# A Mamba-2 scan followed by top-1 routed experts: six routing groups, late scatters spread over two jobs, the first job begun ahead of the last rows

## The chip, the core and the metric

The kernel runs on one core of a Trainium2 chip. The metric is the device time of one execution in microseconds (us); lower is better. PE is the matrix engine (TensorE; its weight loads are listed apart as PEld), DVE the vector engine, ACT the scalar engine, POOL the general-purpose engine (GpSimd), SP the engine that here only issues DMAs. PE's results go to PSUM; SBUF is the on-chip working memory and HBM the large one.

## What is computed

```
# Mamba-2 scan, batch 4, 8 heads, sequence 768, head 32, state 16, in chunks:
y[i] = sum_{j<=i in chunk} (C_i . B_j) * decay(i,j) * x_j  +  (C_i . state) * decay(i)
state = decay_chunk * state + sum_j B_j x_j * decay(j..end)

x = y as (3072 tokens, 256)
logits = x @ w_gate                       # 8 experts
e = argmax(logits); gate = softmax(logits)[e]
out = gate * ( relu(x @ w1[e]) @ w2[e] )  # 256 -> 1024 -> 256
```

## The kernel before

The program has two parts. The first, the scan, works on 24 units of 128 tokens, two to a step, in a loop over twelve steps `d`. The second, the experts, works on jobs: eight jobs of 256 tokens, one to each expert, and then four pairs of smaller jobs for the tokens that did not fit. Between them stands the routing: each token's row (its 256 values, logits by parts, token number) is scattered into the HBM tensor `x_hbm`, at a place in its expert's region, and every job loads its rows from there.

The order on every engine is the order in which the code is written; no scheduler changes it. Each engine runs its own list in order and waits by semaphores for the others.

One step `d` of the scan does this on PE: the state's part of the output (`y_old`), the chunk's part (`y_own`, one matmul for each head, its right side the masked scores `M` that DVE makes in `weigh`, its left side `xp` that POOL makes in `scaled_x`), and the scores of the next step (`scores`). ACT copies the output from PSUM (`turned`, tile `yT`). One step later `rows` turns it back to rows of tokens on PE and `rows_out` and `logits_of` (DVE) write rows and logits. For the last two steps, 10 and 11, `rows` stands behind the loop, before the first job.

A routing group is a number of units that are ranked together. `RGS` gives the sizes, `CUT` the number of groups that the first scatters belong to; the last group is scattered late. When a group's logits are known, `choose` and `count` mark the experts (DVE and POOL), `rank` counts places on PE in the next step, and `ranked` (DVE) writes the places `pos`. `place(k)` scatters unit `k`: an indirect DMA that POOL issues (line 414), with a one-element memset of the tile `spare` (line 413) ahead of it where `apart` is set. The list `todo` holds the units that wait for it; the loop takes units from it at fixed points of a step.

`m_load(i)` loads a job's rows: five DMAs that SP issues, into `xb` (four) and `lt`. They read `x_hbm`, so they wait for every scatter ahead of them to land. `m_xT(i)` transposes `xb` on DVE into `xT`. `m_h(i)` makes the 1024 hidden values in eight blocks `f`, two matmuls each on PE into one of four PSUM buffers, and a relu on ACT from there into `hT`; after each block it calls `between(f)`, which holds the other work of that time. `m_y(i)` makes the two 128-token halves of the output on PE; ACT scales each by its gate (`put`, tile `yo`) and POOL scatters it to the output (line 553). `load_w(e, u, q)` loads a quarter of an expert's weights through SP. `over` (in job 1) counts all groups, and `empty_rest` scatters empty rows behind the last ones.

Of the kernel before, what the change touches and what calls it, by code (L numbers as in the profile page):

```python
# [23 lines left out]
ND = NP * NC  # L24
NU = 2 * ND
AMIN = 0.75
RGS = [4, 4, 4, 4, 8]
CUT = 4
LAST = len(RGS) - 1
R0 = [sum(RGS[:i]) for i in range(len(RGS))]  # L30
# [17 lines left out]
def ssd_then_moe(ctx, tc, xs_in, ae_in, wgx, w_gate, w1, w2, gx, gb, gc, ga, out):  # L48
    nc = tc.nc
# [152 lines left out]
    def load_w(e, u, q):  # L202
        n = KT * F // 4
        nc.sync.dma_start(out=w_sb[e][u][:, q * n:q * n + n], in_=(w1, w2)[u][e, :, q * n:q * n + n])
# [213 lines left out]

    def place(k, apart=True):
        to_places(rt[grp[k]][:, k - R0[grp[k]], :], pos[:, k:k + 1], apart)  # L420
# [136 lines left out]
    def put(p, mid, gt, dve):  # L557
        yo = mo.tile([128, DM], FP32, name="yo", bufs=3)
        if dve:
            nc.vector.tensor_scalar(out=yo, in0=p, scalar1=gt, scalar2=None, op0=ALU.mult)  # L560
        else:
            nc.scalar.mul(yo, p, gt)  # L562
        put_out(yo, mid)
# [6 lines left out]
    def m_y(i, pp):  # L570
        e = jobs[i][1]
        for t in range(2 - jobs[i][0]):
            p = y_next()
            for f in range(FT):
                nc.tensor.matmul(p, lhsT=ex[i]["hT"][:, f, 128 * t:128 * t + 128],  # L575
                                 rhs=w_sb[e][1][:, f * DM:f * DM + DM], start=(f == 0), stop=(f == FT - 1))
            put(p, ex[i]["lt"][:, t], ex[i]["g"][:, t:t + 1], i >= E - 1)

# [122 lines left out]
    with tc.manual_schedule():  # L701
# [36 lines left out]
        wq = [0, 0, 0, 0, 1, 2, 3, 4, 5, 6, 7, 8]  # L738
        for d in range(ND):
# [7 lines left out]
            per = 3 if d == 8 else 2  # L747
            while todo and d == 10:
                place(todo.pop(0))
# [4 lines left out]
            if todo and d < 10:  # L754
                place(todo.pop(0), False)
                if d == 8:
                    place(todo.pop(0))
            if d + 1 < ND:
                for s in range(2):
                    masked_C(2 * d + 2 + s)  # L760
                    scaled_x(2 * d + 2 + s, nc.gpsimd)
            faded(d)
            if k >= 0:
                if d < ND - 1:
                    rows(k)
# [35 lines left out]
            if k >= 0 and d < ND - 1:  # L801
                rows_out(k)
                if d == 4:
                    take_totals(1)
            if d == 0:
                route_consts()
            if k >= 0 and d < ND - 1:
                logits_of(k)
# [12 lines left out]
            if d == 9:  # L821
                for _ in range(2):
                    place(todo.pop(0))
            if d == 10:
                m_load(0)
                m_load(1)
            if d == 9:
                weakest()
        rows(ND - 2)
# [6 lines left out]
        for e, u in ((1, 1), (2, 0), (2, 1)):  # L836
            for k in range(4):
                load_w(e, u, k)
        rows(ND - 1, Y)
        rows_out(ND - 2)  # L840
        logits_of(ND - 2)
        m_xT(0)
        rows_out(ND - 1, Y)
        logits_of(ND - 1)
        choose(LAST)
        count(LAST)
        for i in range(E):
            def between(f):
                if f == 1:
                    ex[i]["g"] = gates(ex[i]["lt"], 2)  # L850
                if i == 0:
                    if f == FT // 2:
                        rank(LAST)
                        ranked(LAST)
                        for k in range(R0[LAST], NU):
                            place(k)
                        m_load(2)
                        m_load(3)
                    return
                if f != FT // 2:  # L860
                    return
# [20 lines left out]
            if i < E - 1:  # L882
                m_y(i, pp)
# [79 lines left out]
```

## Time and profile before

| | us |
|---|---|
| median of 3 runs | 260.78 (260.47 to 261.06) |
| the profiled execution, its own time | 259.0 |
| its span, first to last instruction | 257.3 |
| PE busy within the span | 240.2 (93%) |
| DVE, ACT, POOL busy | 88.0, 87.7, 84.1 (33 to 34%) |

The page of a profile has each engine's busy time and the span in 40 slices. The timeline lists an engine's instructions in order of time, runs of like ones merged: start, length, engine, line, operation, what is written and read, how many, and in brackets the idle time of the engine ahead of it with what ended it. A matmul of 32-bit values stands as two records. The view by stretches gives for each stretch the busy time of every engine and the clock that PE was granted (1.00 is 2.4 GHz, 0.50 is 1.2 GHz).

### The profile page before, as it was taken

What the parts mean: (1) busy time and instruction counts of PE and PEld (TensorE: products, weight loads), DVE (VectorE), ACT (ScalarE), POOL (GpSimd) and SP (SyncE); (2) the same over time, 40 slices, a digit from 0 to 9 for tenths busy, and PEclk for the clock granted to TensorE, in tenths of its full rate; (3) what the DMA queues carried; (4) which work ended last, traced back from release to release, by engine and by line L of the source; (5) the groups of instructions that cost most, each with busy time, mean ns of one, the idle gap of its engine ahead of it and who ended that gap; (6) DMA issues with size and microseconds to landing.
All of it is one profiled execution on the core that took longest, in us unless ns stands there. A gap on an engine that the chain in (4) does not pass through costs nothing. (4 is left out here: it accounts for less than half of the span.)

```text
span 257.3 us, 5473 instructions
## 1 busy us (share of the span) xinstructions
PE 240.2 (93%) x2013; PEld 202.3 (79%) x2013; DVE 88.0 (34%) x274; ACT 87.7 (34%) x288; POOL 84.1 (33%) x147
## 2 busy tenths in 40 slices
PE   7899899876899879999999999999999999999992
PEld 5677667653688668888888888888998968989781
DVE  5899786845660050202020200106204204222000
ACT  4566647540032041414132322223060431523300
POOL 3745868872018704241413203030201301313031
PEclk9999999996899999999999999999999999999999
DMA  6999968524793389696958597413221200101001
GB/s 172 322 378 323 339 216 247 202 84 103 206 319 122 125 176 327 151 298 146 299 165 265 170 288 176 73 32 73 55 60 29 68 4 16 46 8 38 3 15 43
DMA packets 36407, 39.75 MB, mean 154 GB/s; under 512 B 21947, under 2 KB 23806, under 8 KB 36352
## 3 DMA queue, kind: packets, MB, share of 16 engines
q1 hardware_dynamic: 33360, 30.37, 41.5%
q0 software_dynamic: 2880, 8.66, 8.9%
q8 instruction: 27, 0.44, 0.7%
q14 instruction: 28, 0.23, 0.3%
q10 hardware_dynamic: 112, 0.05, 0.1%
HBM read 29.72 MB, written 9.86 MB: 154 GB/s over the span
## 5 line engine op out<-in xcount | busy, mean ns | idle before, releaser
L540 PE MATMUL h_ps<-xT,w 128*128 128x256 f32 (+3 forms) x512 | 90.1, 335 | 3.3 <-ACT hT L549 2.5
L540 PEld LDWEIGHTS h_ps<-xT,w 128*128 128x128 f32 x512 | 80.6, 190 | 10.9 <-ACT hT L549 2.9
L575 PE MATMUL y_ps<-w,hT 128*128 128x256 f32 x384 | 85.0, 380 | 0.0
L575 PEld LDWEIGHTS y_ps<-w,hT 128*128 128x128 f32 x384 | 72.6, 190 | 10.5 <-issue 0.8
L553 POOL DMA_INDIRECT out_dram<-yo,lt x24 | 23.8, 991 | 76.7 <-ACT yo L562 41.5
L498 DVE TENSOR_REDUCE t_se<-t_sub 128x1 f32<-128x8 f32 (+1 forms) x20 | 3.3, 165 | 115.6 <-ACT t_sub L496 115.6
L549 ACT ACTIVATE hT<-h_ps 128x256 f32<-128x256 f32 x64 | 24.1, 384 | 32.9 <-PE h_ps L540 27.3
L278 DVE TENSOR_TENSOR M<-g,mask 128x1024 f32<-128x1024 f32 x24 | 28.3, 1219 | 12.0 <-PE g L273 7.9
L414 POOL DMA_INDIRECT x_hbm<-rows,pos x24 | 23.8, 992 | 9.6 <-issue 3.6
L615 ACT ACTIVATE hT<-h_ps 128x128 f32<-128x128 f32 (+2 forms) x64 | 18.0, 292 | 23.8 <-PE h_ps L540 23.0
L562 ACT ACTIVATE yo<-y_ps,t_gt 128x256 f32<-128x256 f32 x14 | 6.6, 474 | 43.9 <-PE y_ps L575 36.6
L331 PE MATMUL y<-M,xp 128*32 128x128 f32 x384 | 16.6, 292 | 4.7 <-DVE M L278 3.9
L331 PEld LDWEIGHTS y<-M,xp 128*32 128x32 f32 x384 | 11.4, 115 | 8.5 <-POOL xp L266 3.4
L336 ACT COPY yT<-y 128x512 f32<-128x512 f32 x12 | 7.0, 586 | 29.5 <-PE y L331 27.9
L343 PEld LDWEIGHTS r<-turn,yT 128*128 128x128 f32 x88 | 12.2, 189 | 5.5 <-ACT yT L336 3.9
L343 PE MATMUL r<-turn,yT 128*128 128x160 f32 x88 | 14.9, 312 | 1.7 <-ACT yT L336 1.1
L261 ACT ACTIVATE cm<-xs_n,par 128x128 f32<-128x128 f32 x46 | 15.1, 419 | 1.4 <-DMA xs_n<-in_xs_dram 1.4
L266 POOL TENSOR_TENSOR xp<-xs_n,Ei 128x256 f32<-128x256 f32 x23 | 13.7, 618 | 5.1 <-DVE xp L266 3.5
L273 PE MATMUL g<-cm,xs_n 32*128 32x256 f32 x192 | 15.1, 429 | 0.0
L414 POOL DMA_INDIRECT x_hbm<-zrows,rest x8 | 7.7, 964 | 22.2 <-DMA lt<-x_hbm 14.2
L553 POOL DMA_INDIRECT out_dram<-yh,lh x4 | 3.9, 984 | 32.8 <-ACT yh L589 20.9
L560 DVE TENSOR_SCALAR yo<-y_ps,t_gt 128x256 f32<-128x256 f32 x10 | 4.7, 484 | 23.9 <-PE y_ps L575 23.9
(120 smaller groups left out, 148.6 us busy)
## 6 DMA issues: line engine op xcount, KB each, us to landing
w<-in_w_dram SPq DMA_DIRECT2D x64, 256.0 KB
xs_n<-in_xs_dram SPq DMA_DIRECT2D x20, 320.0 KB
xb<-x_hbm SPq DMA_DIRECT2D x32, 64.0 KB
xb<-x_hbm SPq DMA_DIRECT2D x32, 48.0 KB
xs_n<-in_xs_dram SPq DMA_DIRECT2D x4, 192.0 KB
x_hbm<-zrows SPq DMA_DIRECT2D x1, 672.0 KB
lt<-x_hbm SPq DMA_DIRECT2D x8, 80.0 KB
xs_n<-in_xs_dram SPq DMA_DIRECT2D x4, 128.0 KB
```

The lines of the kernel that those rows point to most:

```text
L261: nc.scalar.mul(t[:, u], st[n]["CT"], par[:, u:u + 1])
L266: eng.tensor_tensor(out=t, in0=st[n]["x"].rearrange("p (h d) -> p h d", d=D), in1=bc(Ei[:, n, :, None], [128, NH, D]), op=ALU.mult)
L273: nc.tensor.matmul(g_ps[:, q, n % 2], lhsT=st[n]["BT"][r], rhs=st[n]["cm"][r].rearrange("p u i -> p (u i)"), start=True, stop=True)
L278: nc.vector.tensor_tensor(out=t, in0=g_ps[:, :, n % 2].rearrange("p q (u i) -> p q u i", u=2), in1=bc(mask[:, None, None, :], [128, 4, 2, ...
L331: nc.tensor.matmul(y_ps[o:o + D, h // 4, CH * s:CH * s + CH], lhsT=st[n]["xp"][:, D * h:D * h + D], rhs=st[n]["M"][:, h], start=first, sto ...
L343: nc.tensor.matmul((to[s] if to else r_ps[:, s])[:, 256 * t:256 * t + 160], lhsT=sd[d]["yT"][:, t, CH * s:CH * s + CH], rhs=turn[:, t].rea ...
L414: s_ = nc.gpsimd.indirect_dma_start(out=x_hbm[:, :], out_offset=bass.IndirectOffsetOnAxis(ap=at, axis=0), in_=row, in_offset=None)
L540: nc.tensor.matmul(p[:, 0:n], lhsT=w[:, c:c + 128], rhs=xT[:, t, 0:n], start=(t == 0), stop=(t == KT - 1))
L549: nc.scalar.activation(ex[i]["hT"][:, f, 0:n], q, func=ACT.Relu)
L553: return nc.gpsimd.indirect_dma_start(out=out[:, :], out_offset=bass.IndirectOffsetOnAxis(ap=tok, axis=0), in_=yo[:, :], in_offset=None, b ...
L575: nc.tensor.matmul(p, lhsT=ex[i]["hT"][:, f, 128 * t:128 * t + 128], rhs=w_sb[e][1][:, f * DM:f * DM + DM], start=(f == 0), stop=(f == FT ...
L615: nc.scalar.activation(ex[i + u]["hT"][:, f, 0:n], q, func=ACT.Relu)
```

## The change

`RGS` is cut into six groups in place of five: the fourth group of four units becomes two groups of two, so that one more `rank` runs, in step 8. Units are taken from `todo` up to three times a step from step 8 on; all 16 units of the first groups are then scattered by the end of step 9. The loads for jobs 0 and 1, and those of the weights of expert 2, are issued behind them at the end of step 9; the second weights of expert 1 are loaded ahead of them. `rows` for step 10 moves into step 11, and the transposition for job 0 too. `rows` for step 11 moves behind the first block of job 0. The eight scatters of the last group, which stood together in job 0, are now in pairs: two behind block 5 of job 0, two behind each of its output halves, and two in job 1, behind a small copy on POOL (`behind`) that reads the third block of its `hT`. The loads for jobs 2 and 3 follow the last pair.

```
-RGS = [4, 4, 4, 4, 8]
-CUT = 4
+RGS = [4, 4, 4, 2, 2, 8]
+CUT = 5
...
+    def behind(ap):
+
+        nc.gpsimd.tensor_copy(spare, ap)
...
-    def m_y(i, pp):
+    def m_y(i, pp, then=None):
...
             put(p, ex[i]["lt"][:, t], ex[i]["g"][:, t:t + 1], i >= E - 1)
+            if then:
+                then()
...
-        wq = [0, 0, 0, 0, 1, 2, 3, 4, 5, 6, 7, 8]
+        wq = [0, 0, 0, 0, 1, 2, 3, 4, 5, 6, 7, 8, 9, 9, 9, 9]
...
-            per = 3 if d == 8 else 2
-            while todo and d == 10:
-                place(todo.pop(0))
             if todo:
                 place(todo.pop(0), False)
             if k >= 0:
                 whole(k)
-            if todo and d < 10:
+            if todo:
                 place(todo.pop(0), False)
-                if d == 8:
-                    place(todo.pop(0))
             if d + 1 < ND:
                 for s in range(2):
                     masked_C(2 * d + 2 + s)
                     scaled_x(2 * d + 2 + s, nc.gpsimd)
+            if todo and d > 7:
+                place(todo.pop(0), False)
             faded(d)
             if k >= 0:
-                if d < ND - 1:
-                    rows(k)
+                rows(k)
...
-            if k >= 0 and d < ND - 1:
+            if d == ND - 1:
+                m_xT(0)
+            if k >= 0:
                 rows_out(k)
...
-            if k >= 0 and d < ND - 1:
+            if k >= 0:
                 logits_of(k)
...
             if d == 9:
-                for _ in range(2):
+                while todo:
                     place(todo.pop(0))
-            if d == 10:
                 m_load(0)
                 m_load(1)
-            if d == 9:
+                for k in range(8):
+                    load_w(2, *divmod(k, 4))
+            if d == 10:
                 weakest()
-        rows(ND - 2)
...
-        for e, u in ((1, 1), (2, 0), (2, 1)):
-            for k in range(4):
-                load_w(e, u, k)
-        rows(ND - 1, Y)
-        rows_out(ND - 2)
-        logits_of(ND - 2)
-        m_xT(0)
-        rows_out(ND - 1, Y)
-        logits_of(ND - 1)
-        choose(LAST)
-        count(LAST)
+        left = list(range(R0[LAST], NU))
+
+        def more_places(n):
+            for _ in range(n):
+                place(left.pop(0))
+
...
                 if i == 0:
-                    if f == FT // 2:
+                    if f == 0:
+                        rows(ND - 1, Y)
+                        rows_out(ND - 1, Y)
+                        logits_of(ND - 1)
+                        choose(LAST)
+                        count(LAST)
+                    if f == 5:
                         rank(LAST)
                         ranked(LAST)
-                        for k in range(R0[LAST], NU):
-                            place(k)
-                        m_load(2)
-                        m_load(3)
+                        more_places(2)
                     return
+                if i == 1 and f == 2:
+                    behind(ex[1]["hT"][0:1, 2, 0:1])
+                    more_places(len(left))
+                    m_load(2)
+                    m_load(3)
...
-                m_y(i, pp)
+                m_y(i, pp, (lambda: more_places(2)) if i == 0 else None)
```

On POOL, in steps 9 and 10: `S` is the state of `whole`, `xp` the product of `scaled_x`, the DMAs of line 414 are the scatters, `rows_134` the fourth group's rows. Before, from the first scatter of step 9 on:

```order
L414 DMA x_hbm<-rows_133,pos 28672x336
L314 TENSOR_TENSOR S<-S,fa 128x128
L266 TENSOR_TENSOR xp<-xs_n,Ei 128x256 x2
L413 MEMSET spare 1x1
L414 DMA x_hbm<-rows_134,pos 28672x336
L413 MEMSET spare 1x1
L414 DMA x_hbm<-rows_134,pos 28672x336
L413 MEMSET spare 1x1
L414 DMA x_hbm<-rows_134,pos 28672x336
L413 MEMSET spare 1x1
L414 DMA x_hbm<-rows_134,pos 28672x336
L314 TENSOR_TENSOR S<-S,fa 128x128
```

Four scatters of the fourth group stand in a row here. The same stretch of POOL in the changed kernel, where `rows_134` and `rows_135` are the two groups of two:

```order
L414 DMA x_hbm<-rows_133,pos 28672x336
L314 TENSOR_TENSOR S<-S,fa 128x128
L414 DMA x_hbm<-rows_134,pos 28672x336
L266 TENSOR_TENSOR xp<-xs_n,Ei 128x256 x2
L414 DMA x_hbm<-rows_134,pos 28672x336
L413 MEMSET spare 1x1
L414 DMA x_hbm<-rows_135,pos 28672x336
L413 MEMSET spare 1x1
L414 DMA x_hbm<-rows_135,pos 28672x336
L314 TENSOR_TENSOR S<-S,fa 128x128
```

The scatters that stood four in a row between `xp` and the next `S` are now three, and one has moved ahead of `xp`.

On PE, from the scores of the last step to the first blocks of job 0 (line 273 is `scores`, 323 `y_old`, 331 `y_own`, 343 `rows`, 540 or 544 a block of `m_h`), before:

```order
L273 MATMUL g<-cm,xs_n 128x256 x8
L323 MATMUL y<-xs_n,S 64x128 x8
L331 MATMUL y<-M,xp 32x128 x16
L343 MATMUL r<-turn,yT 128x160 x4
L343 MATMUL y_ps_1202<-turn,yT 128x160
L343 MATMUL y_ps_1203<-turn,yT 128x160
L343 MATMUL y_ps_1202<-turn,yT 128x160
L343 MATMUL y_ps_1203<-turn,yT 128x160
L540 MATMUL h_ps_1199<-xT,w_0_85 128x256 x2
```

Here all `rows` of steps 10 and 11 (into `r` and into `y_ps`) stand between the last `y_own` and the first block. The same stretch of PE in the changed kernel:

```order
L273 MATMUL g<-cm,xs_n 128x256 x8
L343 MATMUL r<-turn,yT 128x160 x4
L323 MATMUL y<-xs_n,S 64x128 x8
L331 MATMUL y<-M,xp 32x128 x16
L544 MATMUL h_ps_1226<-xT,w_0_85 128x256 x2
L343 MATMUL y_ps_1229<-turn,yT 128x160
L343 MATMUL y_ps_1230<-turn,yT 128x160
L343 MATMUL y_ps_1229<-turn,yT 128x160
L343 MATMUL y_ps_1230<-turn,yT 128x160
L544 MATMUL h_ps_1227<-xT,w_0_85 128x256 x2
```

The `rows` of step 10 have moved ahead of the last `y_old`, and those of step 11 behind the first block.

On POOL in jobs 0 and 1 (line 557 is the scatter of an output half, line 421 the copy of `behind`, `rows_136` the last group), the changed kernel has:

```order
L557 DMA out_dram<-yo,lt 3072x256
L413 MEMSET spare 1x1
L414 DMA x_hbm<-rows_136,pos 28672x336
L413 MEMSET spare 1x1
L414 DMA x_hbm<-rows_136,pos 28672x336
L557 DMA out_dram<-yo,lt 3072x256
L413 MEMSET spare 1x1
L414 DMA x_hbm<-rows_136,pos 28672x336
L413 MEMSET spare 1x1
L414 DMA x_hbm<-rows_136,pos 28672x336
L421 COPY spare<-hT_138 1x1
```

Before, all eight scatters of the last group stood ahead of the first output half; now two do, and six follow it.

## Rows read from the trace of the kernel before

**Rows 1.** Page: busy us, share, instructions of each engine; PE's granted clock in 40 slices

```profile
PE 240.2 (93%) x2013; PEld 202.3 (79%) x2013; DVE 88.0 (34%) x274; ACT 87.7 (34%) x288; POOL 84.1 (33%) x147
...
PEclk9999999996899999999999999999999999999999
```

**Rows 2.** Stretches: length; busy us (instructions) PE, PEld, DVE, ACT, POOL; clock; DMA

```profile
60.00:66.50 6.50, 5.84 (x76) 3.89 (x80) 4.26 (x7) 0.59 (x1) 0.00 (x0) 0.50 0.60 109
...
85.40:95.20 9.80, 7.30 (x36) 6.04 (x35) 2.79 (x20) 2.94 (x9) 3.06 (x5) 1.00 0.62 146
95.20:109.00 13.80, 13.80 (x66) 12.15 (x65) 2.48 (x11) 4.13 (x11) 4.07 (x6) 1.00 0.77 234
```

**Rows 3.** Timeline of PE, end of step 9 to the first job

```profile
51.62 0.18 PE L388 MATMUL r<-base_e,ones_bf 1*128 1x32 bf16 x1
...
52.22 1.06 PE L331 MATMUL y<-M,xp 128*32 128x128 f32 x32
53.21 1.15 PE L273 MATMUL g<-cm,xs_n 32*128 32x256 f32 x16
...
55.60 0.67 PE L323 MATMUL y<-xs_n,S 32*64 32x128 f32 x15
57.35 0.26 PE L323 MATMUL y<-xs_n,S 32*64 32x128 f32 x1 [1.08 <-issue]
60.23 2.21 PE L331 MATMUL y<-M,xp 128*32 128x128 f32 x32 [2.62 <-DVE M L278]
62.37 2.09 PE L273 MATMUL g<-cm,xs_n 32*128 32x256 f32 x16
64.39 1.13 PE L323 MATMUL y<-xs_n,S 32*64 32x128 f32 x16
65.90 1.77 PE L331 MATMUL y<-M,xp 128*32 128x128 f32 x32 [0.38 <-DVE M L278]
67.61 1.35 PE L343 MATMUL r<-turn,yT 128*128 128x160 f32 x8
68.80 1.25 PE L343 MATMUL y_ps<-turn,yT 128*128 128x160 f32 x8
70.88 4.58 PE L540 MATMUL h_ps<-xT,w 128*128 128x256 f32 x20 [0.83 <-DVE xT L509]
```

**Rows 4.** Timeline of DVE: the masked scores of step 10

```profile
58.86 2.36 DVE L278 TENSOR_TENSOR M<-g,mask 128x1024 f32<-128x1024 f32 x2 [4.08 <-remote]
```

**Rows 5.** Timeline of POOL: the first and the last of four scatters in a row

```profile
53.06 1.01 POOL L414 DMA_INDIRECT x_hbm<-rows,pos  x1 [0.88 <-DVE less L432]
...
56.91 0.96 POOL L414 DMA_INDIRECT x_hbm<-rows,pos  x1 [0.21 <-issue]
```

**Rows 6.** Timeline of PE: the hidden blocks of job 1

```profile
85.35 3.62 PE L540 MATMUL h_ps<-xT,w 128*128 128x256 f32 x16
91.46 1.13 PE L540 MATMUL h_ps<-xT,w 128*128 128x256 f32 x4 [2.50 <-ACT hT L549]
```

**Rows 7.** Timeline of ACT: second output half of job 0, first blocks of job 1

```profile
86.78 0.47 ACT L562 ACTIVATE yo<-y_ps,t_gt 128x256 f32<-128x256 f32 x1 [4.20 <-PE h_ps L540]
91.03 0.66 ACT L549 ACTIVATE hT<-h_ps 128x256 f32<-128x256 f32 x2 [3.77 <-remote]
```

**Rows 8.** Timeline of POOL: first, last scatter of last group; last output half

```profile
76.73 1.01 POOL L414 DMA_INDIRECT x_hbm<-rows,pos  x1 [3.56 <-DMA w<-in_w_dram]
...
85.66 0.96 POOL L414 DMA_INDIRECT x_hbm<-rows,pos  x1 [0.21 <-issue]
...
88.23 1.00 POOL L553 DMA_INDIRECT out_dram<-yo,lt  x1 [0.30 <-issue]
```

**Rows 9.** Timeline of SP: the first load for job 2

```profile
88.31 1.91 SPq L474 DMA_DIRECT2D xb<-x_hbm  x4
```

**Rows 10.** DMA queues from 88.3 to 92.3: packets, MB, share of 16 engines

```profile
q1 hardware_dynamic: 1343, 0.34, 46.0%
```

**Rows 11.** Timeline of DVE: the transposition for job 2

```profile
94.73 0.71 DVE L509 STREAM_TRANSPOSE xT<-xb 128x512 f32<-128x512 f32 x1
```

## The prediction, made before the changed kernel was run

> **What bounds the kernel now.** I read the page first. PE is busy for 240.2 of 257.3 us and no other engine for more than 88 [rows 1], so what is to be had lies in PE's own idle time and in its slow clock; one slice of PEclk reads 6, the others 8 or 9. Then the stretches [rows 2]: from 95.2 on a job fills PE wholly (13.80 of 13.80), and between 60.0 and 66.5 the granted clock is 0.50, the lower of the two levels (1.2 GHz). Two places are left: the end of the scan, and job 1 (85.4 to 95.2: 7.30 busy of 9.80).
>
> At the end of the scan [rows 3] PE ends the scores of step 9, of which step 10's `M` is made, at 54.36 (53.21 + 1.15), and DVE could then make that `M`. It starts at 58.86, after 4.08 us idle [rows 4]; the bracket says "remote", so no instruction's end explains the release. PE stalls 1.08 us in the middle of `y_old` and then 2.62 for `M`; the clock is low from about 60 to 66.5. Over the same time POOL issues four scatters back to back, from 53.06 to 57.87, 1.28 apart [rows 5]; DVE resumes 0.99 behind the last one's end.
>
> In job 1 PE has filled its four PSUM buffers by 88.97 and waits 2.50 for ACT [rows 6]. ACT was late: its last output half of job 0 starts at 86.78, though PE had it ready at about 85.5, and its first block of job 1, ready by 86.4 (85.35 and four records of 0.22), starts at 91.03, again "remote" [rows 7]. The late blocks lie beside the end of ten scatters in a row on POOL, eight from 76.73 on and two of the output, done at 89.23 [rows 8]. So both holes have one look: PE has finished, the reader learns of it late, and POOL has just issued a run of scatters. That is an inference from coincidence; it is the weakest step.
>
> **The change, part by part.** *One more group.* Step 8 gets one `rank` more. In step 9 the rank and the sixteen `own` matmuls take 0.60 together (51.62 to 52.22) [rows 3], so it costs between 0 and 0.6 of PE; the rank is the larger part of that stretch, and I take +0.35. `choose`, `count` and `ranked` of small tiles go to DVE, which is busy a third of the time; the wait for PE's scores hides them, and without it they would cost their own time, which is under that of the rank's stretch again. `weakest` on DVE moves one step on, in front of a wait for scores as before: nothing.
>
> *The run of scatters in steps 9 and 10.* Before the run POOL sat idle 0.88 for `pos` [rows 5]. The scatter that is moved ahead of `xp` takes 1.0 and some 0.15, so it uses that idle time and sets the rest back by 0.27; three scatters from 53.33 on, 1.28 apart, end at 56.85 in place of 57.87. If DVE is released 0.99 behind that, `M` starts at 57.84: -1.0. Bounds: 0, if it is not the run that holds it; -3.7 (PE's 1.08 and 2.62), if a shorter run holds nothing.
>
> *Clock, `rows` of step 10, start of job 0.* PE's idle time shrinks only to some 2.7 us with one matmul in it, so I take it that the clock falls as before, for 6.5 us. PE starts `y_own` at 59.23. At the low clock it takes 2.14 and the scores 2.02 (steps between starts in [rows 3]), to 63.4. `rows` of step 10, now here, take 1.19 at full clock (67.61 to 68.80); scores slow from 1.1 to 2.02, so I take 2.2, to 65.6. There the clock is full again: `y_old` 0.6 and `y_own` 1.06, to 67.3. DVE's `M` for step 11, started behind the scores, needs 2.36, done by 65.9, and `xT` 0.71 [rows 11], done by 66.6, so neither is waited for. The first block begins at 67.3; `rows` of step 11 (1.25) lie behind it, and ACT's copy for them is hidden by that block's 0.87. Against 70.88 that is 67.3 + 1.25 - 70.88 = -2.4, of which -1.0 is counted above: -1.4. What covers the moved `rows` is the wait for `M` (0.38, and what of it a full clock would add); at the low clock it covers them only in part, and that is in the sum. Behind `xT` on DVE are queued `rows_out` of steps 10 and 11, for which PE waits only at the rank in job 0, six blocks on.
>
> *Loads.* Those for job 0 still follow the last scatter of the run, so they move by the same 1.0, and now lead two megabytes of weights as they led three. The four quarters for expert 1 go to step 9, where SP has nothing else to do. No term.
>
> *Scatters in jobs 0 and 1.* Six of the eight leave the stretch before the first output half. If a run of ten makes PE's news late, and runs that are broken by output scatters don't, the 2.50 of job 1 goes: -2.5; bounds 0 and -2.5. I take all of it, because PE in job 0 stood beside eight scatters without a gap, and only the end of the run was beside a hole.
>
> *What is late next: the rows of job 2.* Count from T1, the start of job 1. A half of `m_y` is 16 records at 0.216, 3.45 [rows 6], and ACT's 0.47 with some 0.3 for hand-over follows, so the first half of job 0 is with POOL about 2.65 before T1. Output scatter 1.3, two scatters 2.55: POOL is free at T1 + 1.2, when the second half waits already; output 1.3, two scatters 2.55, the copy (no row shows it; between 0 and the 0.30 that stands ahead of an output scatter [rows 8], taken 0.15; its block was ready by about T1 + 3.2), two scatters 2.2 to the second one's end: T1 + 7.4. The load waited 1.69 behind the end of the last scatter (86.62 to 88.31) [rows 8, 9], so it is issued at T1 + 9.1. In 4.0 us from there 0.34 MB had moved [rows 10], and one job's `xb` are 0.25, so they land 3.0 to 4.4 behind their issue, and 6.4 at the latest, when DVE transposed them [rows 11]. `xT` is then there at T1 + 12.8 to 14.2; job 1 ends at T1 + 13.9. Before, there were over 6 us to spare; now there is nothing. I take +0.2, between 0 and +2.3 (with 6.4). The copy holds POOL up, and behind it stand two scatters, and through them the loads for jobs 2 and 3 on SP and `empty_rest` on POOL; the last two have a job's time more.
>
> *The sum:* 0.35 - 1.0 - 1.4 - 2.5 + 0.2 = -4.35. The profiled execution would go from 259.0 to 254.65. The median of the timed runs lies 1.8 above it; the same difference gives 256.4.
>
> **The rivals.** *The clock stays up.* The idle time of 2.50 in job 1 left it at 1.00 [rows 2, 6], and the shortened hole is about as long. Against it: before that hole PE had run dense, here it had run in short pieces. At full clock `y_own` waits for its second `M` (to 60.8), scores 1.1, `rows` 1.2, `y_old` 0.6, then `M` again: the first block at 65.2 and not 67.3. That gives 254.3.
>
> *The hole in job 1 stays.* POOL still issues out, two, out, two, two behind each other across T1, with the same 0.3 between them; only the copy has been put in, and it does not wait. Then 2.3 come back (the 0.2 at job 2 is absorbed): 258.7.
>
> *Neither hole has to do with the run.* What speaks for it: from 76.73 to 85.35 PE kept step beside seven scatters. Then only the rank, the moved `rows` and the start of job 0 count, 0.35 - 1.4 = -1.05, and job 1 keeps its hole: 259.7. The Trainium skill ("SBUF — State Buffer", section "SBUF: two separate sides") would have it so: of the engines only DVE and GpSimd share a port, and PE and ACT never wait on anyone. By that rule both hole terms would be 0; the rows neither bear it out nor refute it, since what is late in [rows 4, 7] is the news of PE's work and not a port.
>
> *Slower: job 2 waits.* If `xT` of job 2 comes 2.6 late, PE stands as long as at 57.6 to 60.2, after which the clock fell. Price: 2.6 - 0.2 for the wait and about 3.2 for 6.5 us at half clock: 262.0. It decides from `xb` landing 6.7 behind its issue, or a POOL chain that is longer by as much (ACT's second half of job 0 held up as at 86.78 is 0.7 of that). For it: no slack is left. Against it: 6.4 was the most the landing took before, and the loads of rows then had weights behind them as now.
>
> **How the numbers follow.** Forecast 0.44, clock up 0.15, hole stays 0.17, no link 0.10, slower 0.14. A measurement here tells about 0.2% (0.5 us) from no change. Faster by over that: the first three and half of the fourth, less 0.04 for what I have mispriced, 0.77; within it 0.08; slower 0.15. The likeliest case alone reaches from 254.9 to 258.3. For 8 in 10 the range takes in the clock's case and the hole's and part of the fourth, and ends short of the slower one: 253.5 to 260.4.
>
> **What would show it.** POOL's three scatters ending near 56.9 and `M` starting within 1 us of it; PEclk near 61; the first block of job 0 directly behind the last `y_own`, at about 67, with `rows` behind it; no idle PE in job 1; the start of job 2 on PE, with or without a wait for `xT`. It is wrong if the wait for `M` keeps its place or grows, or if job 2 starts more than 2 us late.

## The result

| | us |
|---|---|
| median after, 6 runs | 252.59 (251.26 to 253.48) |
| median before, 6 runs beside them | 260.68 (259.51 to 261.49) |
| ratio | 0.9689, 95% interval 0.9653 to 0.9726 |
| the profiled execution of after, its own time; its span | 252.05; 250.3 |

The change makes the kernel 3.1% faster here, 8.1 us where 4.35 were forecast; 252.59 lies 0.9 below the range on record. From profile to profile it is 259.0 to 252.05, so 6.95; the other 1.1 come from the two profiled executions, which lie 1.7 (before, by these runs) and 0.5 us below their medians. Here and below, a ratio is taken without executions that fell far behind the others of their kernel, a median of all of them.

The page of after, busy time of PE and its granted clock in 40 slices (of before: [rows 1]); the low slices near the end of the scan are gone:

```profile
PE 238.3 (95%) x2015; PEld 201.3 (80%) x2015; DVE 88.9 (36%) x279; ACT 87.6 (35%) x288; POOL 84.3 (34%) x147
...
PEclk9999999999999999999999999999999999999997
```

Two stretches of after (length; busy us (instructions) PE, PEld, DVE, ACT, POOL; clock; DMA), to set beside [rows 2]. The clock is 1.00 where it was 0.50, and PE is busy through the whole of the second stretch, the end of job 0 and all of job 1:

```profile
60.00:66.00 6.00, 4.70 (x74) 3.45 (x67) 4.30 (x8) 0.67 (x3) 0.00 (x0) 1.00 0.53 102
...
73.00:94.00 21.00, 21.00 (x100) 18.41 (x100) 3.33 (x24) 5.05 (x14) 10.12 (x19) 1.00 0.36 113
```

PE's timeline from the scores of step 9 to job 2 (of before: [rows 3, 6]): `y_own` of step 10 at 57.61 and not 60.23, in two pieces, the first block of job 0 at 64.85 behind a wait of 1.18 for `xT`, then the rows of step 11 at 65.79, and no idle time after that:

```profile
53.75 1.15 PE L273 MATMUL g<-cm,xs_n 32*128 32x256 f32 x16
...
57.61 0.64 PE L331 MATMUL y<-M,xp 128*32 128x128 f32 x15 [0.83 <-DVE M L278]
58.48 0.90 PE L331 MATMUL y<-M,xp 128*32 128x128 f32 x17 [0.23 <-issue]
...
64.85 1.10 PE L544 MATMUL h_ps<-xT,w 128*128 128x256 f32 x4 [1.18 <-DVE xT L513]
65.79 1.25 PE L343 MATMUL y_ps<-turn,yT 128*128 128x160 f32 x8
66.87 4.48 PE L544 MATMUL h_ps<-xT,w 128*128 128x256 f32 x20
...
80.38 4.48 PE L544 MATMUL h_ps<-xT,w 128*128 128x256 f32 x20
...
84.75 2.84 PE L544 MATMUL h_ps<-xT,w 128*128 128x256 f32 x12
...
94.37 0.92 PE L544 MATMUL h_ps<-xT,w 128*128 128x256 f32 x3
```

DVE's masked scores `M` of step 10 and the transpositions for jobs 0 and 2 (of before: [rows 4, 11]):

```profile
56.23 2.35 DVE L278 TENSOR_TENSOR M<-g,mask 128x1024 f32<-128x1024 f32 x2 [1.64 <-PE r L343]
...
63.99 0.71 DVE L513 STREAM_TRANSPOSE xT<-xb 128x512 f32<-128x512 f32 x1 [1.12 <-DMA xb<-x_hbm]
...
93.60 0.71 DVE L513 STREAM_TRANSPOSE xT<-xb 128x512 f32<-128x512 f32 x1 [5.03 <-DMA xb<-x_hbm]
```

POOL: first and last of the three scatters of steps 9 and 10, then the first output half of job 0 and the last scatter of tokens (of before: [rows 5, 8]):

```profile
54.12 1.01 POOL L414 DMA_INDIRECT x_hbm<-rows,pos  x1 [0.17 <-issue]
...
56.70 0.96 POOL L414 DMA_INDIRECT x_hbm<-rows,pos  x1 [0.21 <-issue]
...
77.87 1.00 POOL L557 DMA_INDIRECT out_dram<-yo,lt  x1 [2.98 <-ACT yo L566]
...
86.99 0.96 POOL L414 DMA_INDIRECT x_hbm<-rows,pos  x1 [0.23 <-issue]
```

SP: the loads for jobs 0 and 2 (of before: [rows 9]):

```profile
59.42 2.86 SPq L478 DMA_DIRECT2D xb<-x_hbm  x4
...
89.57 1.81 SPq L478 DMA_DIRECT2D xb<-x_hbm  x4
```

**Where the 8 us came from.** Three points split the two timelines of PE. (1) `y_own` of step 10: 60.23 to 57.61, so -2.62, although the scores of step 9 begin 0.54 later (53.21 to 53.75). (2) From there to the blocks of job 0, with the rows of step 11 counted in both: 10.65 (60.23 to 70.88) to 8.49 (57.61 to 64.85, and 1.25), so -2.16. (3) From there to job 2: 31.18 (70.88 to 102.06) to 28.27 (94.37 less 66.10), so -2.91, of which 2.50 is the idle time of job 1. Together -7.69 at the start of job 2; at the end of the span -7.0 are left.

### The profile page after: what moved, and what is told of

Its sections match the earlier page's. It is cut to its first block, busy times and chain, and to the rows that moved or that the text cites. A ratio compares the mean times of both kernels' runs of the same rounds, so it can differ in the third digit from the quotient of the medians.

```text
span 250.3 us, 5484 instructions
## 1 busy us (share of the span) xinstructions
PE 238.3 (95%) x2015; PEld 201.3 (80%) x2015; DVE 88.9 (36%) x279; ACT 87.6 (35%) x288; POOL 84.3 (34%) x147
## 5 line engine op out<-in xcount | busy, mean ns | idle before, releaser
L331 PE MATMUL y<-M,xp 128*32 128x128 f32 x384 | 15.4, 275 | 2.5 <-DVE M L278 1.6
L331 PEld LDWEIGHTS y<-M,xp 128*32 128x32 f32 x384 | 10.5, 109 | 5.1 <-issue 3.2
```

Of the source, the lines that this page charges most:

```text
L331: nc.tensor.matmul(y_ps[o:o + D, h // 4, CH * s:CH * s + CH], lhsT=st[n]["xp"][:, D * h:D * h + D], rhs=st[n]["M"][:, h], start=first, sto ...
```

## The experiments

They ran on five chips, here A to E, and those of one chip share its runs of the kernel before. The chip turned out to be half of the answer. Ratios are to the kernel before, with 95% intervals:

| chip | before, median | kernels: ratio (interval) |
|---|---|---|
| A | 248.76 | groups_only 1.0106 (1.0062 to 1.0150), late_only 1.0018 (1.0000 to 1.0035), start_only 1.0136 (1.0094 to 1.0178), rows_first 1.0109 (1.0065 to 1.0153) |
| B | 259.13 (1 run) | defer_four 261.03 us, busy_four 262.03 us (1 run each) |
| C | 260.23 | after_again 0.9762 (0.9681 to 0.9844), groups_alone 0.9850 (0.9780 to 0.9920), late_alone 0.9898 (0.9845 to 0.9951), start_alone 0.9870 (0.9793 to 0.9947) |
| D | 248.33 | after_third 1.0115 (1.0081 to 1.0149), undo_groups 1.0171 (1.0109 to 1.0234), undo_late 1.0181 (1.0148 to 1.0214), undo_start 1.0084 (1.0041 to 1.0128) |
| E | 259.00 | after_fourth 0.9793 (0.9723 to 0.9864), filled 0.9840 (0.9770 to 0.9909), rows_first_again 0.9768 (0.9697 to 0.9840); before_again 260.37 us (1 run) |

The theory was that PE's news (that a piece of work of PE is done, for which another engine waits) comes late while POOL issues a run of scatters, at step 10 and in job 1; the rival, that the order of the work alone explains the gain.

### One part at a time, chip A

The three parts of the change, each put alone into the kernel before, and the changed kernel with its last rows ahead of job 0. groups_only:

```diff
-RGS = [4, 4, 4, 4, 8]
-CUT = 4
+RGS = [4, 4, 4, 2, 2, 8]
+CUT = 5
...
-            while todo and d == 10:
-                place(todo.pop(0))
...
+            if todo and d > 7:
+                place(todo.pop(0), False)
             faded(d)
```

> The kernel before with the six groups, the new order of scatters in steps 8 to 10 and the new places of the loads, nothing else. Theory R (a run of scatters on POOL holds back the news of PE's work, and a shorter run holds it less): M of step 10 starts on DVE before 57.5, PE idles under 1.5 us ahead of y_own, the granted clock stays at 1.00, job 0 starts near 66 and not 70.88, and job 1 keeps its 2.5 us hole: about 256, -4.7. Theory N (the holes have nothing to do with the run): M starts at about 58.9 again, the clock falls, time within 1 us of before, 260.7. As the prediction had it (hole shorter by 1.0, clock falls all the same, one more rank): 260.

late_only:

```diff
-                    if f == FT // 2:
+                    if f == 5:
                         rank(LAST)
                         ranked(LAST)
-                        for k in range(R0[LAST], NU):
-                            place(k)
+                        more_places(2)
...
+                if i == 1 and f == 2:
+                    behind(ex[1]["hT"][0:1, 2, 0:1])
+                    more_places(len(left))
```

> The kernel before with the eight late scatters spread over jobs 0 and 1, nothing else. Theory R: the end of the scan is as before (M of step 10 near 58.9, low clock for some 6 us), job 1 has no idle PE, job 2 starts with its xT just there: 258.3, -2.4. Theory N: the hole in job 1 stays, 260.7, or the rows of job 2 come late on top of it.

start_only:

```diff
-                if d < ND - 1:
-                    rows(k)
+                rows(k)
...
+            if d == ND - 1:
+                m_xT(0)
...
+                    if f == 0:
+                        rows(ND - 1, Y)
+                        rows_out(ND - 1, Y)
```

> The kernel before with rows of step 10 in step 11, the transposition for job 0 in the loop and rows of step 11 behind the first block of job 0, nothing else. Both theories: the hole at step 10 and the low clock stay, rows of step 10 then run partly at the low clock; first block at about 68.3, so 68.3 + 1.25 - 70.88 = -1.3: 259.4. The hole of job 1 stays.

rows_first (the changed kernel, edited):

```diff
+        rows(ND - 1, Y)
+        rows_out(ND - 1, Y)
...
-                    if f == 0:
-                        rows(ND - 1, Y)
-                        rows_out(ND - 1, Y)
```

> The changed kernel with rows of step 11 put back ahead of the first block of job 0, nothing else. In the changed kernel PE idles 1.18 us for xT ahead of that block, and rows of step 11 need ACT's copy, there at 64.4: rows would run from 64.4 to 65.7, in the wait for xT, and the first block follow at 65.7, where the second one now starts at 66.87 less the 0.87 of a block = 66.0. So 0.3 faster or the same, 252.3; if the order mattered as the prediction had it (rows behind the block hide a copy), 0.8 slower, 253.4.

Measured: nothing gains, and the expectations for the three parts missed. The late scatters alone change the time by 0.2% (interval 0 to 0.35%), the other three cost 1.1 to 1.4%, and the kernel before takes 248.76 us here, 12 less than in the first measurement. Two timelines say why. First PE in late_only, whose scan is that of the kernel before:

```profile
54.54 0.64 PE L331 MATMUL y<-M,xp 128*32 128x128 f32 x16 [0.49 <-DVE M L278]
...
62.94 5.45 PE L544 MATMUL h_ps<-xT,w 128*128 128x256 f32 x24 [1.10 <-DVE xT L513]
...
77.41 4.48 PE L544 MATMUL h_ps<-xT,w 128*128 128x256 f32 x20
...
81.78 2.84 PE L544 MATMUL h_ps<-xT,w 128*128 128x256 f32 x12
```

Its four scatters, from 51.17 to 55.98 and 1.27 apart, are the same run as [rows 5]:

```profile
51.17 1.01 POOL L414 DMA_INDIRECT x_hbm<-rows,pos  x1 [0.16 <-issue]
...
55.02 0.96 POOL L414 DMA_INDIRECT x_hbm<-rows,pos  x1 [0.22 <-issue]
```

`y_own` of step 10 waits 0.49 for its second `M`, where [rows 3] has 2.62 behind a stall of 1.08, and job 1 stands still nowhere. So this chip doesn't have the holes. What binds is the chain from the last scatter by the load to `xT`: PE waits 1.10 for it. Now PE in groups_only: the rows are ranked later, the last scatter ends at 56.81 (late_only 55.98), `xT` comes later, PE waits 2.74, and the first twenty records of job 0 take 6.27 in place of 4.58 [rows 3], the first of them at the lower clock:

```profile
60.94 1.25 PE L343 MATMUL y_ps<-turn,yT 128*128 128x160 f32 x8
64.92 6.27 PE L540 MATMUL h_ps<-xT,w 128*128 128x256 f32 x20 [2.74 <-DVE xT L509]
```

In start_only PE ends its last `y_own` at 59.74 and just waits longer, 3.95, and the clock falls there too. In rows_first the wait is 2.02 and the clock stays up; but this profile, of 248.93, is the fastest of its four runs (median 251.22).

### Is it the scatters? Chip B

defer_four, the kernel before with the four scatters of steps 9 and 10, and the loads for jobs 0 and 1 behind them, put off until the `M` of step 11 is made:

```diff
-            while todo and d == 10:
-                place(todo.pop(0))
-            if todo:
+            if todo and d < 10:
                 place(todo.pop(0), False)
...
-                for _ in range(2):
-                    place(todo.pop(0))
-            if d == 10:
+            if d == 11:
+                behind(st[22]["M"][0:1, 0, 0:1])
+                while todo:
+                    place(todo.pop(0))
                 m_load(0)
```

> The kernel before, with the run of four scatters of steps 9 and 10 put off until behind the masked scores of step 11, and the loads for job 0 behind them; the rest of the order as before. It loses time at the start of job 0, since its loads come some 10 us later; what is read is the hole at step 10. Theory R: M of step 10 starts within 0.3 us of the end of the scores (about 54.6 and not 58.9), PE idles under 1 us there and the clock stays at 1.00. Theory N: M starts near 58.9 all the same and the clock falls.

busy_four, the same with 13 fills of 128x336 in the place of the scatters:

```diff
             if d == 9:
+                for _ in range(13):
+                    nc.gpsimd.memset(idle_t, 0.0)
```

> The same kernel as the last, with 13 memsets of 128 x 336 (0.38 us each by the one of the trace, 4.9 in all) in the place of the four scatters, so that POOL is as busy and xp of step 11 as late as before, but issues no DMA. If it is the scatters (theory R): as without the four, M of step 10 near 54.6, clock 1.00. If it is POOL being busy, whatever it does: M near 58.9, hole and low clock as before.

In time both are slower than the kernel before, since the rows of job 0 now come late (PE waits 5.98 and 6.11 for `xT`). The place in question is `y_own` of step 10; PE in defer_four:

```profile
55.79 0.65 PE L331 MATMUL y<-M,xp 128*32 128x128 f32 x16
56.59 0.64 PE L331 MATMUL y<-M,xp 128*32 128x128 f32 x16 [0.15 <-DVE M L278]
```

and in busy_four:

```profile
56.20 0.64 PE L332 MATMUL y<-M,xp 128*32 128x128 f32 x16
57.23 0.64 PE L332 MATMUL y<-M,xp 128*32 128x128 f32 x16 [0.39 <-DVE M L279]
```

with POOL filled beside it:

```profile
52.14 5.61 POOL L826 MEMSET idle_t<- 128x336 f32 x13
```

The hole is gone in both: idle times of 0.15 and 0.39, where [rows 3] has 3.70. POOL was busy without a gap from 52.14 to 57.75 in busy_four, so a busy POOL by itself holds nothing up; what does is the scatters. Whether it is their issue or their transfers isn't shown, since the fills make neither. In job 1, where the ten scatters were left as they are, PE still stands 2.53 us in busy_four, which shows that B is a chip with the holes, and 0.35 and 1.01 in defer_four. One run each, and the kernel before has no profile on this chip, but the difference at step 10 is an order of magnitude. The Trainium skill ("SBUF — State Buffer", section "SBUF: two separate sides") has it that at SBUF's ports PE never waits on another engine. busy_four agrees: beside the fills PE is idle only those 0.39, for `M`. On the news of PE's work that section of the Trainium skill says nothing, and the news is what is late.

### One part at a time, chip C

The same three kernels and the changed one on a chip where the kernel before takes 260.

> The changed kernel itself, beside its parts on the same chip. Theory (two holes: TensorE's completion news is held back while GpSimd issues several scatters in a row, once at steps 9 and 10 and once in job 1): on a chip where the kernel before shows both holes and takes 259 to 261 us, the change gives -7 to -9 us (ratio 0.965 to 0.973); on a chip where the kernel before takes about 249 us and shows neither hole, it gives -1 to +3 us. Rival (the gain is the order of the work and has nothing to do with late news): -5 us or more on any chip.

> The kernel before with the new rank groups, the new places of the scatters in steps 8 to 10 and of the loads behind them; the late scatters stay together in job 0 and the end of the scan is as before. Where the holes exist: hole at step 10 goes, job 1's stays, so -2.5 to -5 us; what it gets back is limited because TensorE then waits for the loaded rows of job 0. Rival (only the order counts): the same +3 us as on the chip without holes.

> The kernel before with the late scatters alone spread over two jobs. Where the holes exist: the hole of 2.5 us in job 1 goes and nothing else, -1.5 to -3 us (ratio 0.988 to 0.994). Rival (job 1's idle time has another cause): 0, as on the chip without holes.

> The kernel before with the rows of step 10 inside step 11 and the last rows behind the first block of job 0; groups and scatters as before. Where the holes exist: both stay, the rows that are moved fill none of them, and job 0 begins up to 1.4 us earlier, -1.5 to 0 us. Rival (this part carries most of the gain, since job 0 begins earlier): -4 us or more.

Measured by the ratios: -2.4% (6.2 us) for the whole, -1.5% (3.9) for the groups, -1.0% (2.7) for the late scatters, -1.3% (3.4) for the start; by medians -7.0, -5.0, -3.7 and -4.1. The whole comes out just short of the 7 to 9 expected, the groups and, by the ratio, the late scatters as expected; the start gains over twice what was allowed for. The parts add up to 3.8%, 1.6 times the whole (by medians 12.8 us, 1.8 times). With intervals of 0.5 to 0.8 to either side of each ratio, an overlap is likely and not settled. That the same three edits lose or gain nothing on chip A puts out the rival that the order alone gives the gain. The rows tell which part removes what. In groups_alone DVE starts `M` of step 10 at 56.20, in the middle of its run of scatters, and the clock stays up; job 1 still stands 1.06 and 0.30. In late_alone the first hole is all there, and job 1's 2.50 is gone (20 records from 83.58 without a wait, the next at 87.90); yet the clock, behind the same hole as in the kernel before, doesn't fall in this execution:

```profile
55.37 1.35 PE L343 MATMUL r<-turn,yT 128*128 128x160 f32 x8 [1.26 <-issue]
...
57.66 0.26 PE L323 MATMUL y<-xs_n,S 32*64 32x128 f32 x1 [0.35 <-issue]
58.37 0.41 PE L323 MATMUL y<-xs_n,S 32*64 32x128 f32 x2 [0.45 <-issue]
59.84 0.65 PE L331 MATMUL y<-M,xp 128*32 128x128 f32 x16 [1.05 <-DVE M L278]
60.97 0.64 PE L331 MATMUL y<-M,xp 128*32 128x128 f32 x16 [0.49 <-DVE M L278]
```

In start_alone both holes are there (DVE idle for 4.16 ahead of `M`, job 1 stands 2.53). `y_own` of step 10 is slow, but the clock is full again when the moved rows run, and PE goes from the last `y_own` into job 0 without a wait:

```profile
58.90 2.21 PE L331 MATMUL y<-M,xp 128*32 128x128 f32 x32 [1.06 <-DVE M L278]
61.04 1.61 PE L273 MATMUL g<-cm,xs_n 32*128 32x256 f32 x16
62.58 1.35 PE L343 MATMUL r<-turn,yT 128*128 128x160 f32 x8
...
64.46 1.41 PE L331 MATMUL y<-M,xp 128*32 128x128 f32 x32
65.85 1.10 PE L540 MATMUL h_ps<-xT,w 128*128 128x256 f32 x4
```

This is where the expectation for the start went wrong: the moved rows do fill waits. Without them (before_again, on chip E below) PE waits 0.85 for the first `M` of step 11 and 0.83 for `xT`; here it waits for neither. With the groups beside them the moved rows meet a new bound, the landing of job 0's rows; PE in after_again, on the same chip:

```profile
66.87 1.10 PE L544 MATMUL h_ps<-xT,w 128*128 128x256 f32 x4 [1.83 <-DVE xT L513]
```

So the parts can overlap in two things: each shortens or happens to escape the stretch at the lower clock, which can be won back only once, and groups and start together end in a wait for rows that neither has alone (0 in start_alone; in groups_alone 0.83, as before, with `xT` made only when DVE came to it). Both are inferred from one profile each, and how the overlap divides between them isn't shown.

late_only and late_alone are the same kernel, on chips of the two kinds. Like instructions take the same time on both (scores 1.15, `rows` 1.35, a scatter 0.96 to 1.01), and PE's scores start within 0.12 us of each other up to 33 us. Behind that the chip with the holes falls back: 2.55 us by the scores of step 9 (50.42 and 52.97), half of it in `y_own` of step 8, which stops twice, for 0.35 and 0.30, where chip A doesn't stop; 6.43 by `y_own` of step 10, 6.17 at the first block of job 0 and again at job 2. So the chips don't differ in all durations, and the hole at step 10 is the larger part of what they differ in here, not all of it.

### One part undone, chip D

Three kernels that each lack one part; their edits are the three above taken back.

> The changed kernel, as the measure for the three that each undo one part. On a chip where the kernel before takes 259 to 261 us: 252 to 253.5 us.

> The changed kernel with the old rank groups and the old places of scatters and loads in steps 8 to 10. Theory (late news beside a run of scatters): the hole at step 10 returns, about 3 us of idle time on TensorE before the own outputs of step 10; the rows of job 0 come at the same time as before, so that part of the hole only replaces the wait for them: +1 to +3 us against the changed kernel. Rival (groups and start fill the same gap): 0.

> The changed kernel with the eight late scatters together in job 0 again. Theory: job 1 stands still for 1 to 2.5 us again, +1 to +2.5 us against the changed kernel. Rival (the spread scatters only help when the first hole is there): 0.

> The changed kernel with the rows of step 10 and the last rows ahead of job 0 again. Theory: job 0 is bound by the landing of its rows, so moving TensorE's work from one side of that wait to the other gives at most the length of the wait: 0 to +1.3 us against the changed kernel. Rival (this part's 4 us alone are its own): +3 us or more.

Chip D is of A's kind: the kernel before takes 248.33, and **the changed kernel is slower by 1.15%**, 2.96 us. That is inside the -1 to +3 us that the expectation for after_again gave for a chip without the holes, and puts out its rival, a gain of 5 us or more on any chip. My expectations for the three were for the other kind, and were not put to the test. What the traces give is the reason for the loss. PE in after_third:

```profile
58.52 1.40 PE L331 MATMUL y<-M,xp 128*32 128x128 f32 x32
64.28 1.76 PE L544 MATMUL h_ps<-xT,w 128*128 128x256 f32 x4 [4.36 <-DVE xT L513]
65.84 2.31 PE L343 MATMUL y_ps<-turn,yT 128*128 128x160 f32 x8
```

and its clock there (columns as in [rows 2]):

```profile
60.00:66.00 6.00, 1.72 (x5) 1.45 (x6) 1.77 (x4) 0.58 (x1) 0.00 (x0) 0.88 0.71 140
```

PE ends the last `y_own` at 59.92 and waits 4.36 for `xT`. Behind the wait the first block takes 1.76 and the rows 2.31, where after has 1.10 and 1.25: 1.72 us for the clock. late_only (chip A) has the scan of the kernel before. Against it three things are later here: the chain to `xT` by 1.26 (transposition for job 0 from 63.43, there from 62.17), the rows of step 11, which lie behind the first block and not in the wait, by 1.25, and the clock's 1.72. That makes 4.23, and job 2 begins 4.08 later (95.44 and 91.36). These are profiles on two chips, so it is a reading and not a measured price. Undoing the groups or the start changes nothing that can be told (1.0171 and 1.0084 against 1.0115, intervals that overlap). Undoing the late scatters costs about 0.7% (the two intervals just touch), but not by a hole: job 1 doesn't stand still in any of the four. Its four runs show a mean clock of 0.982 to 0.983, those of after_third 0.988 to 0.993; why it is lower stays open. In undo_start a wait of 1.97 was enough for the clock to fall; PE there (twenty-four records took 5.45 in late_only):

```profile
62.59 7.13 PE L544 MATMUL h_ps<-xT,w 128*128 128x256 f32 x24 [1.97 <-DVE xT L513]
```

### The wait and the last rows, chip E

filled, the changed kernel with work in the wait for job 0:

```diff
+        for _ in range(7):
+            nc.tensor.matmul(H[(turn_no[0] + 1) % 4][:, 0:256], lhsT=w_sb[0][0][:, 0:128],
+                             rhs=w_sb[0][0][:, 0:256], start=True, stop=True)
         for i in range(E):
```

> The changed kernel, as the measure for the other two. 252 to 253.5 us where the kernel before takes 259 to 261, about 251.3 where that takes 248 to 249.

> The kernel before, for its rows on this chip. Theory (the two kinds of chips differ in one thing, late news of TensorE beside runs of scatters): where it takes 248 to 249 us, M of step 10 is not held back, TensorE stands still neither there nor in job 1, waits 0.5 to 1.5 us for the rows of job 0, and its clock does not fall; where it takes 259 to 261 us, the rows are those shown of it. Rival (the chips differ in all durations): the rows of the fast chip are shorter in general.

> The changed kernel with seven products of 128x128 by 128x256 on resident weights (0.45 us each by the 4.48 us of ten, 3.1 us in all, their result overwritten) between the last own outputs and the first block of job 0. Theory (the clock pays for the wait): where TensorE waits 4.4 us there and the clock falls, the wait shrinks to about 1.2 us, the clock stays up and the first block and the rows behind it take 1.10 and 1.25 us again: -1 to -1.7 us against the changed kernel though 3.1 us of work are added. Where the wait is 1.2 to 1.8 us and the clock stays up: +1.3 to +2 us. Rival (the clock has no part in it): 0 in the first case.

> The changed kernel with the last rows ahead of the first block of job 0 again. Theory: they take 1.25 us out of the wait, so job 0's blocks come 0.9 to 1.25 us earlier wherever the wait is at least that long (1.18 and 1.83 us in two profiles of the changed kernel, 4.4 us in a third): -0.5 to -1.5 us against the changed kernel. Rival (what stands behind the first block covers the news of its rows): 0 or above.

Chip E is one with the holes again (259.00). filled costs 1.2 us against after_fourth (253.91 and 252.73, with overlapping runs), close to the +1.3 expected where the clock is up anyway; the case in which it would have told the clock apart didn't come up, and stays open. rows_first_again is 0.8 us faster than after_fourth (251.92 and 252.73) with overlapping runs: the sign is as expected, the size isn't settled, and on chip A it lost 1.1% against before, as the changed kernel did on D. before_again shows both holes of the kernel before once more, and one thing that the first profile hadn't: the clock falls behind the hole of job 1 too. PE in before_again:

```profile
55.27 1.35 PE L343 MATMUL r<-turn,yT 128*128 128x160 f32 x8 [1.25 <-issue]
...
59.74 0.71 PE L331 MATMUL y<-M,xp 128*32 128x128 f32 x16 [1.06 <-DVE M L278]
60.87 1.08 PE L331 MATMUL y<-M,xp 128*32 128x128 f32 x16 [0.42 <-DVE M L278]
61.88 1.97 PE L273 MATMUL g<-cm,xs_n 32*128 32x256 f32 x16
...
65.30 0.65 PE L331 MATMUL y<-M,xp 128*32 128x128 f32 x16 [0.85 <-DVE M L278]
...
70.28 4.58 PE L540 MATMUL h_ps<-xT,w 128*128 128x256 f32 x20 [0.83 <-DVE xT L509]
...
90.83 2.03 PE L540 MATMUL h_ps<-xT,w 128*128 128x256 f32 x4 [2.46 <-ACT hT L549]
...
92.75 3.61 PE L540 MATMUL h_ps<-xT,w 128*128 128x256 f32 x12
```

Four records take 2.03 where [rows 6] has 1.13, and twelve 3.61 where after has 2.84: the hole of 2.46 costs some 1.7 us more than itself in this execution, and in start_alone and busy_four, after 2.53, nothing. That may be one source of the spread of the kernel before on this kind of chip (255.92 to 260.59 on E).

## Why the prediction was wrong, step by step

*The mechanism* was right as far as this: scatters hold back the news of PE's work (busy_four against before_again), and on a chip with the holes the change shortens the first and removes the second. The rival "neither hole has to do with the run" falls on chips B, C and E. On D even its price, a gain of 1.05, is too kind. But that scatters follow each other at the same pace isn't enough to hold it back. In after POOL issues eight of them one behind another, from 77.87 to 87.95 and 1.27 to 1.44 apart, two of them for the output, and ACT takes the blocks of job 1 as PE makes them (81.44, 82.31, 83.17); the ten before, which ended at 89.23, held it to 91.03. The -2.5 for job 1 came out; the reason given for it, that output scatters break the run, may hold, but no experiment tests it apart, and what about a run holds the news back stays open.

*The release of `M`* is the first step that failed. It was set at 0.99 behind the run's end, so 57.84. The run of three didn't end at 56.85 but at 57.66, since it began at 54.12 and not at 53.33, and yet `M` started at 56.23, while the second scatter was being issued (55.43 to 56.39). On four profiles with four scatters `M` did start 0.99 to 1.08 behind the run's end (of before, late_alone, start_alone and before_again); with three it never did (56.20 in groups_alone, 57.15 in after_again with a run that ended at 59.33). The offset was right for what it was read from and no law. Term: -1.0 forecast; -2.62 measured for `y_own`, which contains the +0.54 by which the scores came later. The news isn't prompt now either: `M` starts 1.33 behind the end of the scores (54.90), where it was 4.50 before and is 0.06 in after_third, on a chip without the holes. What that leaves ahead of `y_own` and in it is 0.83 and 0.23 of idle time. Why three scatters let the news of the scores through and four don't stays open: the scores end 1.3 to 1.5 us behind the start of the run of four and 0.7 to 0.8 behind that of three.

*The clock* is the second step that failed. "I take it that the clock falls as before" was chosen over the rival with 0.15; the first block came at 64.85, the rival had 65.2, and its 254.3 was the nearest time on the list. The argument for the fall was "2.7 us of idle time"; what remained was 1.06 in two pieces, so the step failed by the one before it. Of the 2.45 by which the first block came ahead of the forecast (64.85, not 67.3), 1.62 are the earlier `y_own` (57.61, not 59.23); behind it 2.01 were won, most of it by the full clock, and 1.18 lost again in the wait for `xT`. That it could have gone either way even with the hole in place is shown by late_alone (no fall) and before_again (fall) behind idle times that agree, piece by piece, to 0.07.

*The loads for job 0* were to move by 1.0 and be hidden (`xT` done by 66.6). They moved by 0.19 (59.61 to 59.42), as the run's end did by 0.21, and with PE early they became the bound: 1.18 us of waiting in after, 1.83 in after_again, 1.20 in after_fourth, 4.36 in after_third. The prediction had no rival in which the chain from scatter to `xT` binds; on chips A and D it is the one that PE waits for, and by the reading of after_third it is, with the clock behind the wait, what turns the sign. This is the most instructive gap: every step on PE was priced, and the chain that ran beside it was checked against PE's old times only.

*The rows behind the first block*, 1.25, and the block's cover for them came as forecast (65.79, no idle time behind). *One more group*: +0.54 at the scores of step 9, within its bounds of 0 to 0.6, though two idle pieces of 0.19 and 0.31 just ahead of them may be part of it. *Job 1*: -2.5 forecast and measured; late_alone has it without the other parts, the rival "the hole stays" is out on the chips with the holes. *Job 2*: the count from T1 was right almost to the digit: issue at T1 + 9.19 (9.1 forecast), landing 4.03 behind it (3.0 to 4.4), `xT` ready at T1 + 13.93 (12.8 to 14.2), and PE starts 0.06 later without a wait. The slower rival, decided by 6.7 behind the issue, didn't come.

*From profile to median*: 1.8 was added as for before; it was 0.54. That is 1.2 of the 3.8 by which the forecast missed.

## What to carry to other kernels

When a wait on the main engine is removed, look for the chain that runs beside it and ask when that one ends: here the gain stopped at the landing of the next job's rows, and where the wait had never existed, starting earlier only lengthened another wait and dropped the clock. Keep indirect scatters off the stretches in which other engines wait for TensorE's news, or spread them; what spacing is enough isn't known from these runs. And measure such a change on more than one chip: the same two kernels differ by -3.1% and +1.2%.

## What the runs showed of the chip

- There are chips on which the kernel before takes 248.3 to 248.8 us and others on which it takes 259.0 to 260.7; on the first, the same run of four scatters, 51.17 to 55.98, holds up nothing. Nothing in the kernel differs. The same kernel (late_only and late_alone) keeps step on both to within 0.12 us up to 33 us, and what it loses on the second, 6.17 us, it has lost by the first block of job 0; what differs in the chips is open.
- Thirteen fills in a row on POOL hold up nothing where four scatters in a row cost PE over 3 us. Yet eight scatters one behind another, spread over jobs 0 and 1 (77.87 to 87.95 in after), cost it nothing.
- The clock fell behind waits of PE of 2.74, 3.95, 4.36, 4.45, 4.51, 5.98 and 6.11 us and stayed up behind 1.18 and 1.83; between, it did both (1.97 and 2.46 fall; 2.02, 2.50 and 2.53 no fall). In after_third the first block and the rows behind it took 1.72 us more at the lower clock.
